# A routed choice in single slots, rows fetched earlier, and the last product of an expert turned ahead of the next hidden layer

## The chip, the cores and the metric

The kernel runs on one core of one Trainium2 chip. The metric is the time of one launch on the device, in microseconds (us); lower is better. Engines are named as the profile names them: PE (matrix products; PEld is its weight load), DVE (vector), ACT (scalar), POOL (GpSimd) and SP, which here only issues DMAs.

## What is computed

Three layers run one after the other on 1536 tokens of width 512 (2 batches of 768 tokens):

```python
# 1. attention inside clusters: 8 heads of 64, 16 clusters per head
q_assign = argmax(q_n @ c_n.T); k_assign = argmax(k_n @ c_n.T)
scores = where(q_assign[:, None] == k_assign[None, :], q @ k.T / 8, -1e9)
x = softmax(scores) @ v                      # -> 1536 x 512
# 2. one of 8 experts for every token, 512 -> 1024 -> 512
e = argmax(x @ w_gate)
y = softmax(x @ w_gate)[e] * sigmoid(x @ w_output_gate[:, e]) * (relu(x @ w1[e]) @ w2[e])
# 3. dense layer, 512 -> 2048 -> 512
h = y @ w_in
out = (h * sigmoid(1.702 * h)) @ w_out
```

## The kernel before, in words

**Attention** (about 25 to 262 us of the span) is a loop of 96 steps written out by hand (line 939 on), one step for 128 queries of one head. In a step PE makes the scores (L515, L516), DVE finds the row maximum (`nm`, L518), ACT takes the exponential (L524), PE transposes the result (L532) and ACT and DVE copy one half each out of PSUM (`pT`, L537 and L539). Every engine works through its instructions in the order in which the program issues them.

**Routing** is a Python generator, `route(gi)` (L606 on), run for three groups of tokens: the 768 of the first batch, then twice 384 of the second. The loop takes it one `yield` further four times in a step, so its small DVE instructions fall between those of attention. For group 0 it also makes the *choice* (L670 to L690): 18 DVE instructions on tiles of 128x8 or less that find the largest expert of the first half, its number and its first row (`soon`), and how many of its tokens, at most `FIRST` = 128, are worked on early. The rank sums (`prk`) lie in a PSUM slot that PE's `pox` (L586) uses next; the slot comes free with `dest` (L691). After that POOL scales the rows by the gate (L725) and scatters them to the tensor `xd` (an indirect DMA, L730).

**The early expert.** `soon_at` (L921) says at which attention step its parts are issued: the number and the row (`soon_ids`, step 75), the weights in twelve DMAs (`soon_weights`, L760, steps 84 and 87), the 128 rows (`soon_rows`, L782, step 87, behind the last of the weights), and their transposes (`soon_x`, L790, step 91). All DMAs named so far but POOL's are issued by SP in this order. The products (L806, L816) run behind attention, at 267 to 284 us.

**Experts** (284 to 463 us). A conditional branch for overflowing experts (L1233, not taken here) comes first. Then experts 0 to 7 run with 304, 256, 224, 208, 192, 176, 160 and 128 rows. The rows of expert 0 are fetched behind the branch by `win_start(0, True)` (L1323; L1105) in three DMAs of 128, 128 and 48 rows; `win_x` transposes them (L1118) and splits them into a high part (ACT, L1122) and a low part (DVE, L1123). An expert has eight steps `g`, `c = g % 8`. In a step:

- a weight tile is split: ACT casts the high part (L1048), POOL subtracts the low part (L1051); where `g % 4 == 3`, DVE does that instead of POOL (`split_low`);
- `win_h` makes the hidden layer on PE (L1130 to L1132, or L1134 and L1135 where a tile holds high and low rows side by side). ACT copies half of the sums (`hs`, L1140), DVE adds the halves (L1141), ACT applies relu and gives the high part (`ht`, L1155), DVE gives the low part (L1158, `low`);
- `win_y` makes the second product of the step two before (L1134, L1135). With the last one of an expert, which falls into the step `c == 1` of the next expert, `win_out` adds the output (`hs` and `room`, four times L1140 and L1141), writes `yth` on ACT (L1182) and `ytl` on POOL (L1183).

The order of issue on DVE in such a step is: the total of `h` (L1141), the four of `room` if there are any, `split_low`, then `low`.

**The dense layer** (463 to 731 us) keeps PE busy throughout.

Of the kernel before, what the change touches and what calls it, by code (L numbers as in the profile page):

```python
# [9 lines left out]
F32 = mybir.dt.float32  # L10
# [4 lines left out]
ALU = mybir.AluOpType  # L15
# [4 lines left out]
B, H, S, D = 2, 8, 768, 64  # L20
C = 16
NT = B * S
DM = H * D
E = 8
# [22 lines left out]
def attention_moe_ffn(ctx: ExitStack, tc: tile.TileContext, q, k, v, centroids, w_gate, w_og, w1, w2, w_in, w_out, out):  # L47
    nc = tc.nc
    const = ctx.enter_context(tc.tile_pool(name="const", reuse_waits="tile", bufs=1))

    def f32(ap):
        return ap.bitcast(F32)
# [553 lines left out]
    def route(gi):  # L606
# [4 lines left out]
        def new(nm, shape, dt=F32):  # L611
            return one.tile(shape, dt, name=f"{nm}{gi}")
# [54 lines left out]
        if gi < len(GROUPS) - 1:  # L667
            lk = new("lk", [128, E])
        if gi == 0:
            nc.vector.scalar_tensor_tensor(lk, part, float(E), rev8, op0=ALU.mult, op1=ALU.add)  # L670
            lm, lv = new("lm", [128, 1]), new("lv", [128, E])
            nc.vector.tensor_reduce(lm, lk, op=ALU.max, axis=AX.X)
            nc.vector.tensor_scalar(soonh, lk, lm, None, op0=ALU.is_equal)
            yield
            nc.vector.tensor_tensor(lv, soonh, part, op=ALU.mult)
            nc.vector.tensor_reduce(ngone, lv, op=ALU.add, axis=AX.X)
            nc.vector.tensor_scalar(ngone, ngone, float(FIRST), None, op0=ALU.min)
            yield
            nc.vector.tensor_scalar(gone, soonh, ngone, None, op0=ALU.mult)
            nc.vector.scalar_tensor_tensor(sbase, gone, -1.0, ebase, op0=ALU.mult, op1=ALU.add)  # L680
            nc.vector.scalar_tensor_tensor(srev8, gone, -float(E), rev8, op0=ALU.mult, op1=ALU.add)
            yield
            nc.vector.tensor_tensor(lv, soonh, ebase, op=ALU.mult)
            nc.vector.tensor_reduce(span[:, 1:2], lv, op=ALU.add, axis=AX.X)
            nc.vector.tensor_tensor(span[:, 0:1], span[:, 1:2], ngone, op=ALU.subtract)
            yield
            nc.vector.tensor_tensor(lv, soonh, iota8, op=ALU.mult)
            nc.vector.tensor_reduce(lm, lv, op=ALU.add, axis=AX.X)
            nc.vector.tensor_copy(soon[:, 0:1], lm[0:1])
            nc.vector.tensor_copy(soon[:, 1:2], span[0:1, 0:1])  # L690
        nc.vector.tensor_tensor(dest, rk, sbase[:, None, :].to_broadcast([128, nj, E]), op=ALU.add)  # L691
        if gi == len(GROUPS) - 2:
            nc.vector.scalar_tensor_tensor(lk, part, float(E), srev8, op0=ALU.mult, op1=ALU.add)
        yield
# [223 lines left out]
    slots.update({21: 3, 27: 1, 75: 1, 80: 1, 81: 2, 86: 3, 87: 2, 92: 2, 93: 2})  # L918

    weights = soon_weights()  # L920
    soon_at = {75: [soon_ids], 84: [lambda: next(weights)], 87: [lambda: next(weights), soon_rows], 91: [soon_x]}  # L921

    fixed = ExitStack()
    fixed.enter_context(tc.manual_schedule())
# [170 lines left out]
    def win_load(ex_row, n, one_tile=False, pieces=False):  # L1095
        nr = -(-n // 128)
        if one_tile:
            x = hp.tile([128, 2 * CAP], F32R, name="ht", tag="ht")[:, None, :DM].bitcast(F32)
        else:
            x = xp.tile([128, WR, DM], F32, name="xr", tag="xr", bufs=1)  # L1100
        d = {"n": n, "nr": nr, "x": x}
        for r0 in range(0, nr, 1 if pieces else nr):
            m, p = (1, min(128, n - r0 * 128)) if pieces else (nr, 128)
            row = nc.s_assert_within(ex_row + r0 * 128, 0, E * NT - 128, skip_runtime_bounds_check_because="inside the rows of an expert") if r0 else ex_row
            x = nc.sync.dma_start(out=d["x"][:p, r0:r0 + m], in_=xd[bass.ds(row + FIRST, m * p)].rearrange("(r p) c -> p r c", p=p)).ins  # L1105
            need(x, scatters)
        return d

    def win_x(d, r):
        if r == 0:  # L1110

            side = CAPS.index(d["n"]) % 2 if d["n"] in CAPS else 0
            d["t"] = xp.tile([128, 8 * CAPS[side]], F32R, name="t", tag=f"t{side}", bufs=1)[:, :8 * d["n"]].rearrange("p (k n) -> p k n", k=4)
        m = min(128, d["n"] - r * 128)
# [5 lines left out]
        hi = d["t"][:, :, n + r * 128:n + r * 128 + m]  # L1120
        src = pt.rearrange("p (k n) -> p k n", k=4)[:, :, :m]
        nc.scalar.copy(hi, src)  # L1122
        nc.vector.tensor_tensor(d["t"][:, :, r * 128:r * 128 + m], src, f32(hi), op=ALU.subtract)  # L1123

    def product(ps, n, w_hi, w_lo, t, first, last):

# [81 lines left out]

    xp = cx.enter_context(tc.tile_pool(name="xp", reuse_waits="tile", bufs=2))
    hp = cx.enter_context(tc.tile_pool(name="hp", reuse_waits="tile", bufs=3))  # L1210

    wins = {}
# [10 lines left out]
    relus[1]()  # L1223
    low_parts.append(split_pair(ekeys[1], 0, None, nc.vector, True))
    some(100)
    for f in low_parts:
        f()
    trips = nc.values_load_multi_w_load_instructions(trip, min_val=0, max_val=NOV)[1][0]
# [91 lines left out]
            ahead[g] = ph  # L1320

    with tc.manual_schedule():
        win_start(0, True)  # L1323
        loads_to(6)
        banks.clear()
        banks.extend([(ps_m, "m"), (ps_t, "pt"), (ps_t, "pt"), (ps_a, "po")])
        for r in range(wins[0]["nr"]):
            win_x(wins[0], r)
        n_, half = order[2]
        split_pair(ekeys[n_], half)  # L1330
        exps += experts(plan[:, 1:E])
        dense_load(2)
        win_start(1)
        loads_to(7)
        G = E * 8
        hq = deque()
        for g in range(G + 2):
            e, c = divmod(g, 8)
            nxt = wins.get(e + 1)
            r = c - (7 - nxt["nr"]) if nxt else 0  # L1340
            split_low = low = out_low = None
            if g + 3 < len(order):
                n_, half = order[g + 3]
                split_low = split_pair(ekeys[n_], half, None, nc.vector if g % 4 == 3 else nc.gpsimd, g % 4 == 3)
                loads_to(g + 7)
            if nxt and 0 <= r < nxt["nr"]:
# [15 lines left out]
            if g >= 2:  # L1362
                g0, ht = hq.popleft()
                e0, c0 = divmod(g0, 8)
                win_y(wins[e0], ("e", e0, c0 // 2), c0 % 2, ht, c0 == 0, c0 == 7)
                if c0 == 7:

                    low_end = S // 8 + (e0 and (LEAST + (e0 - 1) * ((NT - FIRST - LEAST) // (E - 1))))
                    col = nc.s_assert_within(offs[e0], low_end, NT if e0 else FIRST, skip_runtime_bounds_check_because="a sum of counts")
                    out_low = win_out(wins[e0], col, True, nc.vector if e0 == E - 1 else None)  # L1370
            if split_low:
                split_low()
            for f in (low, out_low):
                if f:
                    f()
            dense_step(min(5 * e + max(0, c - 2), 40) + 3 * min(max(0, g - 61), 2))
            if g < G:
                if c == 0 and e and e + 1 < E:
                    win_start(e + 1)
                if g == 2:  # L1380
                    offs = nc.values_load_multi_w_load_instructions(plan[:, E:], engines=[ACT_E, DVE_E, POOL_E], min_val=0, max_val=NT)[1]
# [111 lines left out]
```

## Time and profile before

| | us |
|---|---|
| median of 3 runs (lowest, highest) | 731.31 (730.92, 732.39) |
| profiled execution | 733.72 |
| its span, first to last instruction | 732.0 |
| busy in the span: PE, DVE, ACT, POOL | 703.2, 458.1, 393.0, 264.4 |
| mean granted clock of PE | 0.985 of full speed |

PE is busy for 96% of the span, so the stretches in which it waits or runs at a lower granted clock are what can be won without taking work away. A time in brackets at the end of a row of a timeline is how long the engine had been idle before, and what released it. A number behind x is how many instructions a row stands for.

### The profile page before, as it was taken

The numbers are of one execution on the slowest core, as the hardware profiler recorded it, in microseconds if no ns is written. First come the engines' busy times: TensorE is split into PE (matmuls) and PEld (weight loads), VectorE is DVE, ScalarE is ACT, GpSimd is POOL, SyncE is SP. The second block draws the span as 40 slices with busy tenths as digits, with TensorE's granted clock in tenths as the row PEclk, the third lists the DMA queues.
The fourth block names the chain that finished last, engine by engine and source line by source line (L and its number), as shares of the span: only waits on it lengthen the run. The fifth ranks groups of instructions, "written<-read, shape, count | busy, mean of one in ns | idle before, by whom it ended". The sixth has DMA issues, their size and how long they took to land.

```text
span 732.0 us, 12543 instructions
## 1 busy us (share of the span) xinstructions
PE 703.2 (96%) x4522; PEld 580.2 (79%) x4522; DVE 458.1 (63%) x886; ACT 393.0 (54%) x789; POOL 264.4 (36%) x219
## 2 busy tenths in 40 slices
PE   8999999998999898999999897999999999999996
PEld 6776776776866678999999887888888888888885
DVE  6969788889888774344554545687655657232322
ACT  7767675675666544556777676544534344222120
POOL 2230330312750013755978889222432212020202
PEclk8999999999899999999999999999999999999999
DMA  6778969637274427766477776132643211010101
GB/s 195 171 189 266 238 216 293 142 121 173 69 200 141 174 86 255 230 215 215 161 254 243 236 224 222 59 116 86 68 73 41 81 59 56 1 58 1 58 0 58
DMA packets 70594, 105.18 MB, mean 144 GB/s; under 512 B 9648, under 2 KB 48304, under 8 KB 70528
## 3 DMA queue, kind: packets, MB, share of 16 engines
q1 hardware_dynamic: 67584, 95.94, 45.9%
q0 software_dynamic: 2944, 8.40, 3.0%
q8 instruction: 37, 0.61, 0.4%
q14 instruction: 29, 0.24, 0.1%
HBM read 70.46 MB, written 14.69 MB: 116 GB/s over the span
## 4 chain that ended last, share of the span: by engine, by line
PE 33%; issue 16%; ACT 5%; DVE 3%; POOL 2%; DMA 1%; POOLq 0%; ACTq 0%; DVEq 0%
PE ph L1317 4%; PE ph L1318 4%; PE ph L1319 4%; PE py L1412 3%; PE py L1411 3%; PE py L1410 3%; PE py L1134 3%; ACT w L1048 3%; PE ph L1134 3%; PE ph L1135 1%; PE py L1135 1%; DVE w L1051 1%; DMA raw<-in_moe_w_dram 1%; POOL out_dram L1421 1%; ACT hs L1140 1%
## 5 line engine op out<-in xcount | busy, mean ns | idle before, releaser
L1051 POOL TENSOR_TENSOR w<-raw,w 128x1024 fp32r<-128x1024 f32 x51 | 125.6, 2482 | 39.3 <-ACT w L1048 38.9
L518 DVE TENSOR_REDUCE nm<-sp 128x1 f32<-128x768 f32 x96 | 91.6, 955 | 16.2 <-PE sp L516 14.1
L1395 DVE TENSOR_TENSOR sg<-ph,sg 128x512 f32<-128x512 f32 x48 | 33.2, 691 | 99.7 <-ACT sg L1394 97.5
L524 ACT ACTIVATE P<-sp,nm 128x768 f32<-128x768 f32 x96 | 87.2, 908 | 11.3 <-DVE nm L518 10.6
L532 PEld LDWEIGHTS pt<-ident,P 128*128 128x128 f32 x576 | 66.4, 143 | 28.1 <-issue 17.5
L532 PE MATMUL pt<-ident,P 128*128 128x128 f32 x576 | 84.3, 280 | 4.0 <-ACT pT L537 2.1
L1394 ACT ACTIVATE sg<-ph 128x512 f32<-128x512 f32 x48 | 28.7, 597 | 104.7 <-PE ph L1319 100.3
L1134 PE MATMUL py<-ht,w 128*128 128x512 f32 (+6 forms) x224 | 70.2, 367 | 8.0 <-DVE ht L1158 5.1
L515 PE MATMUL sp<-X,Q 128*128 128x384 f32 x192 | 74.9, 390 | 0.5 <-ACT P L524 0.4
L1412 PE MATMUL py<-w,gl 128*128 128x512 f32 (+1 forms) x194 | 75.2, 387 | 0.0
L1411 PE MATMUL py<-w,gh 128*128 128x512 f32 (+1 forms) x194 | 75.1, 387 | 0.0
L1410 PE MATMUL py<-w,gh 128*128 128x512 f32 (+1 forms) x194 | 75.0, 387 | 0.0
L1317 PE MATMUL ph<-yth,w 128*128 128x512 f32 x192 | 74.8, 390 | 0.0
L1318 PE MATMUL ph<-ytl,w 128*128 128x512 f32 x192 | 74.7, 389 | 0.0
L1319 PE MATMUL ph<-yth,w 128*128 128x512 f32 x192 | 74.7, 389 | 0.0
L1084 POOL TENSOR_TENSOR w<-csq,w 128x512 fp32r<-128x512 f32 x24 | 32.7, 1364 | 115.7 <-ACT w L1083 115.7
L1048 ACT CAST w<-raw 128x1024 fp32r<-128x1024 f32 x68 | 70.5, 1042 | 4.2 <-issue 2.4
L1134 PE MATMUL ph<-t,w 128*128 128x512 f32 (+6 forms) x224 | 69.4, 365 | 0.4 <-DVE ht L1158 0.4
L567 PE MATMUL po<-pT,ld_v 128*32 128x384 f32 x768 | 69.0, 492 | 0.0
L516 PE MATMUL sp<-Z,Q 80*128 80x384 f32 x192 | 66.4, 346 | 0.5 <-DMA Q<-ohT 0.5
L537 ACT COPY pT<-pt 128x384 f32<-128x384 f32 x96 | 45.8, 477 | 36.8 <-PE pt L532 36.8
L539 DVE COPY pT<-pt 128x384 f32<-128x384 f32 x96 | 52.8, 550 | 12.6 <-PE pt L532 12.2
(291 smaller groups left out, 1476.2 us busy)
## 6 DMA issues: line engine op xcount, KB each, us to landing
raw<-in_moe_w_dram SPq DMA_DIRECT2D x64, 512.0 KB, 4.5
raw<-in_moe_w_in_dram SPq DMA_DIRECT2D x16, 512.0 KB, 4.1
raw<-in_moe_w_out_dram SPq DMA_DIRECT2D x16, 512.0 KB, 4.8
xd<-zrow SPq DMA_DIRECT2D x8, 768.0 KB, 5.9
Q<-Hq SPq DMA_DIRECT2D x28, 192.0 KB, 2.7
ew<-in_moe_w_dram SPq DMA_DIRECT2D x9, 384.0 KB, 7.8
ld_q<-in_q_dram SPq DMA_DIRECT2D x8, 384.0 KB, 6.0
ld_k<-in_k_dram SPq DMA_DIRECT2D x8, 384.0 KB, 3.8
```

The source lines that it names most:

```text
L518: nc.vector.tensor_reduce(nm, sp[:, :, :384], op=ALU.max, axis=AX.XY, negate=True)
L524: nc.scalar.activation(P, L["sp"][:, :, :384], AF.Exp, bias=L["nm"], accum_out=L["sm"][:, h, j % 3:j % 3 + 1])
L532: nc.tensor.transpose(pt[:, r * 128:(r + 1) * 128], L["P"][:, n, r * 128:(r + 1) * 128], ident)
L1048: nc.scalar.copy(hi, r)
L1051: (eng or nc.gpsimd).tensor_tensor(lo, r, f32(hi), op=ALU.subtract)
L1134: nc.tensor.matmul(ps[:, :2 * n], w_hi, t, start=first, stop=False)
L1317: nc.tensor.matmul(ph, wa(key, 0, k, i), yth[:, k, cs], start=(k == 0), stop=False)
L1318: nc.tensor.matmul(ph, wa(key, 0, k, i), ytl[:, k, cs], start=False, stop=False)
L1319: nc.tensor.matmul(ph, wa(key, 1, k, i), yth[:, k, cs], start=False, stop=(k == 3))
L1410: nc.tensor.matmul(po[m][:, cs], gh[:, ms], wb(key, 0, i)[:, cs], start=first, stop=False)
L1411: nc.tensor.matmul(po[m][:, cs], gh[:, ms], wb(key, 1, i)[:, cs], start=False, stop=False)
L1412: nc.tensor.matmul(po[m][:, cs], gl[:, ms], wb(key, 0, i)[:, cs], start=False, stop=last)
```

## The change

- **Choice.** `dest` for group 0 is now written first, from the rank sums and `ebase` alone, and the counts are copied from PSUM to `c0`; every instruction of the choice after that stands in a slot of its own, and at the end `gone` is subtracted from `dest`. Two DVE instructions are added. The generator has twelve more `yield`s, three steps' worth.
- **Early rows.** `soon_rows` moves from the end of step 87 to the front of step 84, ahead of the weights; `soon_ids` moves from step 75 to 78.
- **First rows of expert 0.** The DMA of its first 128 rows is issued ahead of the branch (and waits for the scatters of groups 0 and 1 alone); behind the branch one DMA brings the other 176 as two tiles of 88. `xr` gets a pool of its own, `xrp`.
- **Experts.** In the steps `c == 1` from g = 9 to 57 the last `win_y` of the expert before, with its additions, is issued ahead of that step's `win_x` and `win_h`. In every step `low` is issued ahead of `split_low`. `yth` and `ytl` are still issued last.

```diff
@@ route(0)
-            nc.vector.scalar_tensor_tensor(lk, part, float(E), rev8, op0=ALU.mult, op1=ALU.add)
-            lm, lv = new("lm", [128, 1]), new("lv", [128, E])
+            nc.vector.tensor_tensor(dest, rk, ebase[:, None, :].to_broadcast([128, nj, E]), op=ALU.add)
+            lm, lv, c0 = new("lm", [128, 1]), new("lv", [128, E]), new("c0", [128, E])
+            nc.vector.tensor_copy(c0, part)
+            yield
+            nc.vector.scalar_tensor_tensor(lk, c0, float(E), rev8, op0=ALU.mult, op1=ALU.add)
+            yield
             nc.vector.tensor_reduce(lm, lk, op=ALU.max, axis=AX.X)
+            yield
...
+            yield
+            nc.vector.tensor_tensor(dest, dest, gone[:, None, :].to_broadcast([128, nj, E]), op=ALU.subtract)
+        else:
+            nc.vector.tensor_tensor(dest, rk, sbase[:, None, :].to_broadcast([128, nj, E]), op=ALU.add)
@@ soon_at
-    soon_at = {75: [soon_ids], 84: [lambda: next(weights)], 87: [lambda: next(weights), soon_rows], 91: [soon_x]}
+    soon_at = {78: [soon_ids], 84: [soon_rows, lambda: next(weights)], 87: [lambda: next(weights)], 91: [soon_x]}
@@ win_load
+        if pieces:
+            p = (n - 128) // (nr - 1)
+            d["rows"] = [128] + [p] * (nr - 1)
+            rows_of(0, 1, 128, scatters[:-GROUPS[-1][2]])
+            d["rest"] = lambda: rows_of(1, nr - 1, p, scatters)
+        else:
+            rows_of(0, nr, 128, scatters)
@@ ahead of the branch, and behind it
     some(100)
+    win_start(0, True)
     for f in low_parts:
...
-        win_start(0, True)
+        wins[0]["rest"]()
@@ experts
+            turned = c == 1 and 1 < g < G
+            if turned:
+                finish()
             if nxt and 0 <= r < nxt["nr"]:
                 win_x(nxt, r)
...
-            if split_low:
-                split_low()
-            for f in (low, out_low):
+            if g >= 2 and not turned:
+                finish()
+            for f in (low, split_low, *late):
```

`finish` holds what stood at the place of the old `if g >= 2:`: `win_y` of the step two before and, for the last of an expert, the additions of `win_out`.

## Rows read from the trace of the kernel before

**Rows 1.** Waits of PE, whole span: line, releaser, total us, times, longest.

```profile
PE py L1134 <- DVE ht L1158: 5.1, 5, 2.3
PE py L1134 <- DVE room L1141: 2.7, 4, 0.7
PE pxs L790 <- DMA xs<-xd: 2.4, 1, 2.4
PE pxt L1118 <- issue: 1.4, 1, 1.4
```

**Rows 2.** Windows: PE, PEld, DVE, ACT, POOL busy (instructions), clock, DMA share, GB/s.

```profile
170.00:180.00 10.00, 8.51 (x80) 5.45 (x72) 9.44 (x29) 5.00 (x13) 0.56 (x1) 1.00 0.88 214
180.00:190.00 10.00, 9.23 (x49) 7.58 (x53) 8.46 (x28) 4.63 (x10) 3.90 (x3) 0.66 0.07 26
190.00:200.00 10.00, 10.00 (x88) 7.56 (x81) 8.30 (x15) 7.34 (x17) 8.90 (x9) 1.00 0.31 101
```

**Rows 3.** Timeline of DVE around the choice: start, duration, line, operation.

```profile
178.69 0.16 DVE L670 SCALAR_TENSOR_TENSOR lk<-prk,rev 128x8 f32<-128x8 f32 x1
...
179.80 0.55 DVE L539 COPY pT<-pt 128x384 f32<-128x384 f32 x1
...
182.62 0.18 DVE L691 TENSOR_TENSOR dest<-prk,sbase 128x48 f32<-128x48 f32 x1
```

**Rows 4.** Timeline of PE in the same stretch.

```profile
180.31 0.81 PE L532 MATMUL pt<-ident,P 128*128 128x128 f32 x3 [1.01 <-ACT pT L537]
...
182.86 1.44 PE L586 MATMUL pox<-wo,oa 128*128 128x160 f32 x4 [0.45 <-DVE dest L691]
```

**Rows 5.** Timeline of POOL: the last scatter of group 0.

```profile
205.86 1.05 POOL L730 DMA_INDIRECT xd<-xs,di  x1 [0.28 <-POOL xs L725]
```

**Rows 6.** Timeline of SP's queue around the early expert.

```profile
229.19 4.61 SPq L760 DMA_DIRECT2D ew<-in_moe_w_dram  x7
...
239.66 0.34 SPq L782 DMA_DIRECT2D xs<-xd  x1
```

**Rows 7.** Windows where the early rows are waited for, columns as in rows 2.

```profile
246.00:248.00 2.00, 0.00 (x0) 0.00 (x0) 0.80 (x1) 0.12 (x2) 0.00 (x0) 1.00 0.16 58
248.00:254.00 6.00, 5.86 (x41) 3.69 (x42) 3.17 (x5) 2.48 (x5) 0.00 (x0) 0.72 0.00 0
```

**Rows 8.** Timeline of SP's queue behind the branch.

```profile
280.69 1.46 SPq L1105 DMA_DIRECT2D xr<-xd  x3
```

**Rows 9.** Timeline of PE behind the branch.

```profile
284.35 0.96 PE L1118 MATMUL pxt<-ident,xr 128*128 128x128 f32 x7 [0.40 <-PEq L1233]
286.74 0.70 PE L1118 MATMUL pxt<-ident,xr 128*128 128x128 f32 x5 [1.44 <-issue]
287.96 0.41 PE L1130 MATMUL ph<-t,w 128*128 128x304 f32 x1 [0.52 <-ACT t L1122]
```

**Rows 10.** The window behind those, columns as in rows 2.

```profile
288.00:294.00 6.00, 5.64 (x27) 5.42 (x28) 1.15 (x3) 3.58 (x5) 4.90 (x3) 0.72 0.97 321
```

**Rows 11.** Waits of ACT from 345 to 457 us, columns as in rows 1.

```profile
ACT ht L1155 <- DVE ph L1141: 26.1, 42, 2.2
ACT yth L1182 <- DVE room L1141: 2.6, 6, 0.5
```

**Rows 12.** A window late in the experts, columns as in rows 2.

```profile
430.00:451.00 21.00, 17.38 (x133) 16.69 (x133) 11.36 (x24) 14.41 (x32) 19.47 (x9) 1.00 0.66 206
```

**Rows 13.** Timeline of DVE: two of its weight splits and a low part.

```profile
361.18 2.38 DVE L1051 TENSOR_TENSOR w<-raw,w 128x1024 fp32r<-128x1024 f32 x1
363.48 0.38 DVE L1158 SCALAR_TENSOR_TENSOR ht<-ph,ht 128x224 fp32r<-128x224 f32 x1
...
382.60 1.22 DVE L1051 TENSOR_TENSOR w<-raw,w 128x1024 fp32r<-128x1024 f32 x1
```

**Rows 14.** All DVE splits, 345 to 457 us: busy total and mean ns, idle before.

```profile
L1051 DVE TENSOR_TENSOR w<-raw,w 128x1024 fp32r<-128x1024 f32 x11 | 21.7, 1974 | 0.0
```

**Rows 15.** Timeline of POOL: the splits beside the first of rows 13.

```profile
355.35 7.12 POOL L1051 TENSOR_TENSOR w<-raw,w 128x1024 fp32r<-128x1024 f32 x3 [0.70 <-ACT w L1048]
```

More of the change, by code (lines that the diff above doesn't have):

```diff
@@ L669, in route @@
         if gi == 0:
-            nc.vector.scalar_tensor_tensor(lk, part, float(E), rev8, op0=ALU.mult, op1=ALU.add)
-            lm, lv = new("lm", [128, 1]), new("lv", [128, E])
+            nc.vector.tensor_tensor(dest, rk, ebase[:, None, :].to_broadcast([128, nj, E]), op=ALU.add)
[4 more added lines that the diff above has]
+            yield
             nc.vector.tensor_reduce(lm, lk, op=ALU.max, axis=AX.X)
+            yield
             nc.vector.tensor_scalar(soonh, lk, lm, None, op0=ALU.is_equal)
             yield
-            nc.vector.tensor_tensor(lv, soonh, part, op=ALU.mult)
+            nc.vector.tensor_tensor(lv, soonh, c0, op=ALU.mult)
+            yield
             nc.vector.tensor_reduce(ngone, lv, op=ALU.add, axis=AX.X)
+            yield
             nc.vector.tensor_scalar(ngone, ngone, float(FIRST), None, op0=ALU.min)
@@ L679, in route @@
             nc.vector.tensor_scalar(gone, soonh, ngone, None, op0=ALU.mult)
+            yield
             nc.vector.scalar_tensor_tensor(sbase, gone, -1.0, ebase, op0=ALU.mult, op1=ALU.add)
+            yield
             nc.vector.scalar_tensor_tensor(srev8, gone, -float(E), rev8, op0=ALU.mult, op1=ALU.add)
@@ L683, in route @@
             nc.vector.tensor_tensor(lv, soonh, ebase, op=ALU.mult)
+            yield
             nc.vector.tensor_reduce(span[:, 1:2], lv, op=ALU.add, axis=AX.X)
+            yield
             nc.vector.tensor_tensor(span[:, 0:1], span[:, 1:2], ngone, op=ALU.subtract)
             yield
+            nc.vector.tensor_copy(soon[:, 1:2], span[0:1, 0:1])
             nc.vector.tensor_tensor(lv, soonh, iota8, op=ALU.mult)
+            yield
             nc.vector.tensor_reduce(lm, lv, op=ALU.add, axis=AX.X)
+            yield
             nc.vector.tensor_copy(soon[:, 0:1], lm[0:1])
-            nc.vector.tensor_copy(soon[:, 1:2], span[0:1, 0:1])
-        nc.vector.tensor_tensor(dest, rk, sbase[:, None, :].to_broadcast([128, nj, E]), op=ALU.add)
+            yield
+            nc.vector.tensor_tensor(dest, dest, gone[:, None, :].to_broadcast([128, nj, E]), op=ALU.subtract)
+        else:
+            nc.vector.tensor_tensor(dest, rk, sbase[:, None, :].to_broadcast([128, nj, E]), op=ALU.add)
         if gi == len(GROUPS) - 2:
@@ L1099, in win_load, with rows_of @@
         else:
[L1100 to L1103, printed above, removed]
+            x = xrp.tile([128, WR, DM], F32, name="xr", tag="xr")
+        d = {"n": n, "nr": nr, "x": x, "rows": [128] * (nr - 1) + [n - 128 * (nr - 1)]}
+        def rows_of(r0, m, p, names):
             row = nc.s_assert_within(ex_row + r0 * 128, 0, E * NT - 128, skip_runtime_bounds_check_because="inside the rows of an expert") if r0 else ex_row
             x = nc.sync.dma_start(out=d["x"][:p, r0:r0 + m], in_=xd[bass.ds(row + FIRST, m * p)].rearrange("(r p) c -> p r c", p=p)).ins
-            need(x, scatters)
+            for nm in scatters[len(names):]:
+                tc.declare_no_dep(x, nm, reason="an expert with 128 rows in these groups: later tokens have other rows")
+            need(x, names)
+        if pieces:
+            p = (n - 128) // (nr - 1)
+            d["rows"] = [128] + [p] * (nr - 1)
+            assert sum(d["rows"]) == n and LEAST >= 128
+            rows_of(0, 1, 128, scatters[:-GROUPS[-1][2]])
+            d["rest"] = lambda: rows_of(1, nr - 1, p, scatters)
+        else:
+            rows_of(0, nr, 128, scatters)
         return d
@@ L1113, in win_x @@
             d["t"] = xp.tile([128, 8 * CAPS[side]], F32R, name="t", tag=f"t{side}", bufs=1)[:, :8 * d["n"]].rearrange("p (k n) -> p k n", k=4)
-        m = min(128, d["n"] - r * 128)
+        m, r0 = d["rows"][r], sum(d["rows"][:r])
         xs = d["x"][:m, r]
@@ L1119, in win_x @@
         n = d["n"]
-        hi = d["t"][:, :, n + r * 128:n + r * 128 + m]
+        hi = d["t"][:, :, n + r0:n + r0 + m]
         src = pt.rearrange("p (k n) -> p k n", k=4)[:, :, :m]
         nc.scalar.copy(hi, src)
-        nc.vector.tensor_tensor(d["t"][:, :, r * 128:r * 128 + m], src, f32(hi), op=ALU.subtract)
+        nc.vector.tensor_tensor(d["t"][:, :, r0:r0 + m], src, f32(hi), op=ALU.subtract)
     def product(ps, n, w_hi, w_lo, t, first, last):
@@ L1210, in attention_moe_ffn @@
     hp = cx.enter_context(tc.tile_pool(name="hp", reuse_waits="tile", bufs=3))
+    xrp = cx.enter_context(tc.tile_pool(name="xrp", reuse_waits="tile", bufs=1))
     wins = {}
@@ L1340, in attention_moe_ffn @@
             r = c - (7 - nxt["nr"]) if nxt else 0
-            split_low = low = out_low = None
+            split_low = low = None
+            late = []
             if g + 3 < len(order):
@@ L1345, in attention_moe_ffn, with finish @@
                 loads_to(g + 7)
+            def finish():
+                g0, ht = hq.popleft()
+                e0, c0 = divmod(g0, 8)
+                win_y(wins[e0], ("e", e0, c0 // 2), c0 % 2, ht, c0 == 0, c0 == 7)
+                if c0 == 7:
+                    low_end = S // 8 + (e0 and (LEAST + (e0 - 1) * ((NT - FIRST - LEAST) // (E - 1))))
+                    col = nc.s_assert_within(offs[e0], low_end, NT if e0 else FIRST, skip_runtime_bounds_check_because="a sum of counts")
+                    late.append(win_out(wins[e0], col, True, nc.vector if e0 == E - 1 else None))
+            turned = c == 1 and 1 < g < G
+            if turned:
+                finish()
             if nxt and 0 <= r < nxt["nr"]:
@@ L1361, in attention_moe_ffn @@
                 banks.append((ps_h, "ph"))
[L1362 to L1370, printed above, removed]
-            if split_low:
-                split_low()
-            for f in (low, out_low):
+            if g >= 2 and not turned:
+                finish()
+            for f in (low, split_low, *late):
                 if f:
```

## The prediction

> **What bounds the kernel now.** I read the waits of PE first, because PE is busy for 96% of the span and what it does not do elsewhere it does in the dense layer, where it never waits: a microsecond won ahead of that layer reaches the end. The reader is to see four places [rows 1]: the early rows (2.4 us, once), the transposes behind the branch (1.4), and two waits inside the experts, for the low part of `ht` (5.1 in five times) and for `room` (2.7 in four). The list does not show what the granted clock takes. So I read windows next. From 180 to 190 us the clock is 0.66, a loss of 10 x 0.34 = 3.4 us; PE was busy 8.51 of 10 before it, and DVE 9.44 of 10 [rows 2]. From 248 to 254 it is 0.72, 6 x 0.28 = 1.7 us lost, after two microseconds with PE at 0.00 [rows 7]. From 288 to 294 it is 0.72 again, another 1.7 us, behind the branch [rows 10]. In each, parts of the stretch run at 1.2 instead of 2.4 GHz. Last I read the waits of the engines that PE waits for, stage by stage, since a wait of PE may be the shadow of another engine's pace.
>
> **Choice in single slots.** The choice's first instruction starts at 178.69 and `dest` ends at 182.80 [rows 3], 4.1 us; a `pT` copy of 0.55 and a row maximum of nearly 1 us lie between, so the choice costs 2.6 us of DVE in its densest stretch. PE waits there 1.01 us for a chain that starts with a late DVE and 0.45 us for `dest` [rows 4]. The new order writes `dest` at once and copies the counts, so the second wait goes. But the whole 0.45 + 1.01 + 3.4 = 4.9 us cannot be won: DVE itself is idle for only 10 - 8.46 = 1.5 us of that window [rows 2], and it gets two instructions more, about 0.35 us together at the 0.16 and 0.18 us of such ones [rows 3]. If DVE has the same work to do there, the gain ends at 1.5 - 0.35 = 1.2 us. The twelve new slots move a part of it behind 190 us, where DVE is idle for 1.7 us in 10 [rows 2]; that sets the far end at about -2.7. On the other side the longer stretch meets the preparation of the next heads, and one more stall like that of rows 4 costs 1.5 us. I take -1.0 us, close to what DVE's idle time allows, with -2.7 and +1.5 as ends. Three steps later (a step is (262 - 25) / 96 = 2.5 us) come also POOL's scalings and scatters: the last ended at 206.91 [rows 5] and would end near 215, still 14 us ahead of the first DMA that needs them. I cost that at nothing; if POOL's casts for the next heads came late through it, it would be of the order of 0.5 to 1 us.
>
> **Early rows in front of the weights.** Before, SP issues seven and then five weight DMAs from 229.19 and the rows at 239.66 [rows 6]; PE stands until 248.14, 2.41 us, though it could have used them at 245.7. Issued first, at about 229.2, they have 16 us; even the 8.5 us that they took behind the weights would do. The weights are 0.34 us later, and the products that need them come 20 us later. So the 2.4 us go and with them the fall of the clock, 1.7: -4.1 us. DVE has 3.17 of 6 us to do there [rows 7], so it is not late next. If the clock fell all the same, -2.4 would be left.
>
> **First 128 rows ahead of the branch.** PE's last transposes start at 286.74, 1.44 us after the ones before, and the row names no releaser; I take it to be the last of three DMAs that SP issues in 1.46 us from 280.69 [rows 8, 9]. After, one DMA of 0.49 us remains, so the last piece is issued 1.0 us earlier, and the weights in SP's queue behind it too; with 128 rows out of the way I put the gain at 1.4 us, between that 1.0 and the 0.40 + 1.44 that PE waits. The clock's 1.7 us I leave out: waits of 0.5 us for ACT [rows 9] and the start behind the branch stay. New in SP's queue ahead of the branch is a wait for the scatters of groups 0 and 1; behind it stand only transfers that were issued behind the branch. Ends: 0, if PE waited for something else, such as its own instructions, and -3.5 with the clock. A loss of up to 1 us is possible if the new pool lies where attention's tiles are still in use and SP stands.
>
> **The experts.** At first sight all of 5.1 + 2.7 + 0.4 us goes: `low` no longer stands behind the split, and `room` is asked for a whole `win_h` earlier. But from 345 to 457 us ACT waits 26.1 us for DVE's totals, in all 42 steps, 0.62 us each, and no wait of ACT for PE is in that list [rows 11]; PE is busy only 17.38 of 21 us late in it [rows 12]. So the turn ACT, DVE, ACT sets the pace (weight cast, `hs`, total, relu), and PE's waits are its shadow; only what shortens that turn counts. (1) With the last product turned ahead, `yth` no longer waits for `room`: 6 times, 2.6 us [rows 11]. (2) `low` ahead of the split works both ways. A split that finds POOL free takes 1.22 us [rows 13]; one at 361.18 took 2.38, and POOL's third instruction beside it ended at 355.35 + 7.12 = 362.47 [rows 15]: 1.29 us of waiting and 1.09 of work. Its start does not matter then, and behind it the 0.38 us of `low` [rows 13] no longer delays the next total: -0.3 us. A free split instead starts 0.8 us later (relu and `low`), ends 2.0 us after the total, and ACT brings the next half after some 1.7: +0.3. Walked through one by one, the eleven splits (mean 1.97 us [rows 14]) give six gains of 0.2 to 0.3, two zeros and three losses of 0.2 to 0.4: -0.8. Together -3.4; I take -3.0, since POOL, 19.47 of 21 us busy [rows 12], follows ACT closely and takes some back. Ends: -8.2 and +5, both below.
>
> Whether a DVE split beside POOL waits or merely runs slower decides that step. The sum of 1.29 and 1.09 speaks for waiting. The Trainium skill, "SBUF — State Buffer", section "SBUF: two separate sides", has the rule for it: GpSimd and a VectorE instruction with two SBUF inputs take a shared port pair as an exclusive lock for a whole instruction. The row agrees with it. By the rule my -0.8 stands where POOL's instruction is under way, but where POOL's next one has just begun the lock turns against the later start; that is the second rival.
>
> **Sum.** -1.0 - 4.1 - 1.4 - 3.0 = -9.5 us on the profiled execution's 733.72: 724.2. That execution is 2.4 us above the median of the runs, 731.31, so the forecast is 731.31 - 9.5 = 721.8.
>
> **Rivals.** *All of PE's waits in the experts go*: for it speaks that each names the very instruction that is moved, against it that ACT never waits for PE there. The experts then give -8.2, the time 716.6. *The late split meets POOL's next instruction.* POOL's splits follow without a pause (three in 7.12 us, 2.37 each [rows 15]). A split that starts 0.8 us later and just misses its turn waits a full 2.4 us: 0.8 + 2.4 + 1.1 - 1.7 = 2.6 us on the next total, where today it is about 1.97 + 0.38 - 1.7 = 0.65, so +1.95 for each such step. The gains, 6.5 elsewhere and 2.6 for `yth`, are eaten from the fifth of the eight splits that run beside POOL, and with the sixth the kernel is slower. All eight: +15.6 - 2.6 - 6.5 = +6.5, 737.8. Half of them: about +5 in the experts, 730 to 732. Against it speaks that most splits have over 0.8 us of POOL's instruction still ahead of them. *The change does not do what it says*: the choice stalls PE in its new slots and the clock falls there, and PE waits behind the branch for something other than the rows. The first and third parts give nothing: -7.1, 724.2.
>
> **How the numbers follow.** A measurement of this kernel tells about 0.2% (1.5 us) from no change: faster is below 729.8, slower above 732.8. Forecast 0.48; change without its first and third effect 0.20; all waits gone 0.13; half of the splits caught 0.11; all caught 0.08. So faster 0.81, same 0.11, slower 0.08. The range goes from 714.5, under the best rival by a part of the clock behind the branch, to 729.5, where three splits are caught and the choice gives nothing.
>
> **What would show it.** Right: no wait of PE at `pxs` and a full clock from 246 to 254; `pox` waiting for no `dest`; the last transposes some 1.4 us earlier after the branch; no `yth` waiting for `room`; ACT's waits for totals hardly smaller, while PE's named releasers change and its idle time in the experts shrinks by 3, not 8. Wrong: DVE splits over 3 us in most of the eleven; a clock below 1 behind the choice again; a row maximum that PE waits for in the steps behind it; a new wait of SP ahead of the branch.

## The result, and the profile after

The changed kernel takes 722.85 us (median; 722.55 to 724.04), the kernel before, beside it, 731.85: a ratio of 0.9876, with a 95% interval of 0.9857 to 0.9895. It is 9.0 us faster, where 9.5 were forecast. Its profiled execution has a span of 722.3 us against 732.0, 9.7 less. The total hides that two of the four terms were wrong in opposite directions.

To see where the time went, the same instruction is looked up in both traces. First the kernel before, then the changed one: a row maximum of DVE just ahead of the choice, one of step 76 and one of step 84.

```profile
175.32 0.95 DVE L518 TENSOR_REDUCE nm<-sp 128x1 f32<-128x768 f32 x1
210.61 0.94 DVE L518 TENSOR_REDUCE nm<-sp 128x1 f32<-128x768 f32 x1
228.09 0.96 DVE L518 TENSOR_REDUCE nm<-sp 128x1 f32<-128x768 f32 x1
```

```profile
175.78 0.95 DVE L518 TENSOR_REDUCE nm<-sp 128x1 f32<-128x768 f32 x1
206.78 0.94 DVE L518 TENSOR_REDUCE nm<-sp 128x1 f32<-128x768 f32 x1
225.69 0.96 DVE L518 TENSOR_REDUCE nm<-sp 128x1 f32<-128x768 f32 x1 [1.44 <-PE sp L516]
```

The first pair stands 0.46 us apart the wrong way (in the profiles of the kernels below, which are the same up to there, this row stands anywhere from 174.31 to 175.80, so stages are compared by differences). The second is 3.83 us earlier, the third only 2.40: the choice won 4.3 us, and 1.4 of them went back at step 84 in this execution. Next the changed kernel's timeline of PE behind the branch:

```profile
277.41 0.63 PE L1146 MATMUL pxt<-ident,xr 128*128 128x128 f32 x4 [0.40 <-PEq L1263]
278.81 0.45 PE L1146 MATMUL pxt<-ident,xr 88*128 88x88 f32 x3 [0.78 <-DMA xr<-xd]
280.14 0.99 PE L1146 MATMUL pxt<-ident,xr 88*128 88x88 f32 x5 [0.88 <-issue]
281.68 0.62 PE L1158 MATMUL ph<-t,w 128*128 128x304 f32 x1 [0.54 <-ACT t L1150]
```

and, by line, the first and last start of the first products of its dense layer, then the same of the kernel before:

```profile
L1347 PE MATMUL ph<-yth,w x192: 389/389/447, 453.2 to 706.7; 128*128 128x512 f32 x192
```

```profile
L1317 PE MATMUL ph<-yth,w x192: 389/389/447, 462.9 to 716.4; 128*128 128x512 f32 x192
```

Against [rows 9] the first transposes stand at 277.41 instead of 284.35, 6.94 us earlier, and the first product of the experts at 281.68 instead of 287.96, 6.28 earlier: the stretch behind the branch lost 0.7 us, and it was to win. The dense layer starts at 453.2 instead of 462.9. So 9.7 us are won by there, 3.4 of them in the experts, and none behind. The waits of PE in the changed kernel, as in [rows 1], and its windows that answer to [rows 2, 7, 10], columns as there:

```profile
PE py L1162 <- DVE room L1169: 2.0, 2, 1.4
PE sp L516 <- DMA Q<-ohT: 1.9, 2, 1.2
...
PE py L1162 <- DVE ht L1186: 1.1, 3, 0.6
...
PE pxt L1146 <- issue: 0.9, 1, 0.9
PE pxt L1146 <- DMA xr<-xd: 0.8, 1, 0.8
PE ph L1162 <- DVE ht L1186: 0.7, 2, 0.3
```

```profile
180.00:190.00 10.00, 9.35 (x79) 6.80 (x83) 9.72 (x35) 6.86 (x16) 0.00 (x0) 1.00 0.01 2
190.00:200.00 10.00, 10.00 (x87) 8.89 (x77) 9.11 (x18) 7.98 (x20) 6.45 (x6) 1.00 0.15 46
...
240.00:250.00 10.00, 10.00 (x92) 7.05 (x92) 9.08 (x14) 6.33 (x14) 0.00 (x0) 1.00 0.41 142
...
280.00:290.00 10.00, 9.32 (x47) 8.78 (x48) 2.60 (x5) 6.40 (x10) 7.31 (x4) 0.66 0.98 352
```

The reader is to see four things. The wait for the early rows is gone, and the clock is 1.00 where they were waited for. Behind the choice the clock is 1.00 and DVE is busier than before. A new wait for `Q<-ohT` of 1.2 us stands at step 84. And behind the branch PE still stops with no releaser named, and the clock is 0.66 for 10 us, a loss of 3.4 us.

### The profile page after: what moved, and what is told of

Read it like the earlier page. It is cut to its first block, busy times and chain, and to the rows that moved or that the text cites. A ratio compares the mean times of both kernels' runs of the same rounds, so it can differ in the third digit from the quotient of the medians.

```text
span 722.3 us, 12542 instructions
## 1 busy us (share of the span) xinstructions
PE 699.4 (97%) x4522; PEld 577.7 (80%) x4522; DVE 452.2 (63%) x888; ACT 393.0 (54%) x789; POOL 266.4 (37%) x219
## 4 chain that ended last, share of the span: by engine, by line
PE 54%; issue 17%; POOL 7%; DMA 7%; DVE 6%; ACT 6%; SPq 1%; POOLq 0%; ACTq 0%; DVEq 0%
PE po L567 6%; PE pt L532 5%; PE ph L1347 4%; PE ph L1349 4%; PE ph L1348 4%; PE py L1447 3%; PE py L1445 3%; PE py L1446 3%; PE sp L515 3%; PE sp L516 3%; POOL w L1067 3%; PE py L1162 3%; PE ph L1162 2%; ACT w L1064 2%; DMA raw<-in_moe_w_dram 2%
## 5 line engine op out<-in xcount | busy, mean ns | idle before, releaser
L1067 POOL TENSOR_TENSOR w<-raw,w 128x1024 fp32r<-128x1024 f32 x51 | 128.1, 2529 | 38.3 <-ACT w L1064 25.4
```

What stands on the lines that cost most here:

```text
L1067: (eng or nc.gpsimd).tensor_tensor(lo, r, f32(hi), op=ALU.subtract)
```

## The experiments

The other kernels of the table are the changed one with one edit, but for `changed_again`, which has none, and `loads_held_old_rows`, which has two. Times are medians beside runs of the kernel before on the same chip; since those differ from one measurement to the next (731.9 to 733.8), the ratios are what can be compared.

| kernel | us | ratio to before (95%) | span |
|---|---|---|---|
| changed | 722.85 | 0.9876 (0.9857 to 0.9895) | 722.3 |
| changed_again | 723.65 | 0.9868 (0.9838 to 0.9897) | 722.2 |
| no_choice | 726.12 | 0.9903 (0.9871 to 0.9935) | 726.0 |
| no_early_rows | 728.64 | 0.9943 (0.9920 to 0.9967) | 727.1 |
| no_first_rows | 722.19 | 0.9855 (0.9825 to 0.9884) | 720.5 |
| no_branch | 719.47 | 0.9815 (0.9785 to 0.9844) | 718.1 |
| no_turn | 726.74 | 0.9908 (0.9884 to 0.9931) | 725.7 |
| no_low_first | 726.40 | 0.9894 (0.9865 to 0.9922) | 725.0 |
| choice_dest_first | 726.77 | 0.9906 (0.9877 to 0.9934) | 723.8 |
| transposes_ahead | 724.54 | 0.9874 (0.9850 to 0.9899) | 723.4 |
| loads_held | 726.24 | 0.9899 (0.9871 to 0.9928) | 724.3 |
| loads_held_old_rows | 727.91 | 0.9919 (0.9893 to 0.9945) | 729.2 |
| split_earlier | 719.45 | 0.9814 (0.9787 to 0.9842) | 718.7 |

The changed kernel stands at 0.987 in both of its measurements; 0.1% of the ratio is 0.73 us.

**The choice undone.**

```diff
-            nc.vector.tensor_tensor(dest, rk, ebase[:, None, :].to_broadcast([128, nj, E]), op=ALU.add)
...
-            nc.vector.tensor_copy(c0, part)
-            yield
...
+        nc.vector.tensor_tensor(dest, rk, sbase[:, None, :].to_broadcast([128, nj, E]), op=ALU.add)
```

> The changed kernel with the choice as it was before (up to seven DVE instructions in a slot, dest last); all else as changed. Theory of the traces: from the scores of step 64 to those of step 76 the changed kernel gained 4.3 us on the kernel before (3.3 by step 68) and gave 1.4 back at step 84, so without it the clock falls to about 0.66 from 180 to 190 us again, PE waits again for dest, its wait for Q<-ohT at step 84 goes from 1.2 back to about 0.5 us, and the kernel is about 3.2 us slower than the changed one: 726. Theory of the prediction (DVE's own idle time limits the gain): 1.0 us slower, 723.9.

0.3% slower, 2 to 2.6 us; the span is 3.7 longer. PE's timeline behind the choice, and the window:

```profile
183.25 1.97 PE L586 MATMUL pox<-wo,oa 128*128 128x160 f32 x6 [1.28 <-DVE dest L691]
```

```profile
180.00:190.00 10.00, 8.02 (x53) 6.61 (x57) 8.94 (x30) 5.08 (x12) 3.52 (x3) 0.83 0.04 14
```

The waits are back, 1.28 us for `dest` this time, and the clock falls, though for half as long (0.83, not 0.66). The theory of the traces is nearer than the prediction's 1.0 us, which the interval does not exclude.

**The choice with `dest` first, but in few slots** (twelve `yield`s taken out again).

```diff
             nc.vector.tensor_copy(c0, part)
-            yield
             nc.vector.scalar_tensor_tensor(lk, c0, float(E), rev8, op0=ALU.mult, op1=ALU.add)
-            yield
             nc.vector.tensor_reduce(lm, lk, op=ALU.max, axis=AX.X)
...
```

> The changed kernel with dest and the copy of the counts first, but the choice in as few slots as before. Theory A (what counts is that the PSUM slot of the rank sums comes free at once): no wait of PE for dest, a clock near 1 from 180 to 190 us, 722.9 as the changed kernel, and, with POOL's scatters three steps earlier, PE's wait for Q<-ohT at step 84 at 0.5 instead of 1.2 us. Theory B (what counts is that the choice is thinned out): PE waits 1.0 us for pT again, the clock falls, some 2 us slower, 725.

0.3 to 0.4% slower than the changed kernel, as theory B has it, though the intervals overlap at their ends. PE's timeline shows no wait for `dest`, but three for `pT`, and its window a full clock all the same:

```profile
180.47 0.55 PE L532 MATMUL pt<-ident,P 128*128 128x128 f32 x3 [1.00 <-ACT pT L537]
184.03 0.55 PE L532 MATMUL pt<-ident,P 128*128 128x128 f32 x3 [1.16 <-ACT pT L537]
186.49 0.55 PE L532 MATMUL pt<-ident,P 128*128 128x128 f32 x3 [0.87 <-DVE pT L539]
```

```profile
180.00:190.00 10.00, 7.51 (x59) 5.36 (x60) 9.63 (x31) 4.72 (x11) 3.52 (x3) 1.00 0.04 16
```

From the row maximum of step 64 to that of step 76 this kernel takes 33.0 us, the changed one 31.0 and the one with the choice undone 33.9: in these profiles thinning out is worth 2.0 us, the slot that comes free early 0.9. So thinning out counts for more than the PSUM slot. No wait for `Q<-ohT` stands at step 84 here, nor in the other two kernels with few slots; whether the longer choice makes the 1.2 us of the changed kernel is taken up with its second profile.

**The early rows behind the weights again.**

```diff
-    soon_at = {78: [soon_ids], 84: [soon_rows, lambda: next(weights)], 87: [lambda: next(weights)], 91: [soon_x]}
+    soon_at = {78: [soon_ids], 84: [lambda: next(weights)], 87: [lambda: next(weights), soon_rows], 91: [soon_x]}
```

> The changed kernel with the DMA of the early rows behind the early weights again; all else as changed. Theory: PE waits some 2.4 us at the transposes of the early rows and the granted clock falls behind that, 1.7 us: 4.1 us slower than the changed kernel, 727. Rival: the fall of the clock had to do with what came before it, not with this wait: 2.4 us slower, 725.2.

0.7% slower, about 5 us. The wait is 3.2 us (PE has become earlier, the rows have not), and the clock falls; a wait of PE, then the window:

```profile
PE pxs L806 <- DMA xs<-xd: 3.2, 1, 3.2
```

```profile
240.00:250.00 10.00, 6.83 (x50) 4.91 (x49) 4.80 (x8) 3.89 (x8) 0.00 (x0) 0.83 0.30 105
```

3.2 and 10 x 0.17 = 1.7 are 4.9 us. The theory holds, the rival falls.

**The first rows behind the branch again, and the branch left out.**

```diff
-    win_start(0, True)
     for f in low_parts:
...
-        wins[0]["rest"]()
+        win_start(0, True)
...
```

> The changed kernel with the rows of expert 0 fetched by three DMAs behind the branch, as before; all else as changed. Theory of the prediction (the landing of the rows sets the last transposes): they come about 1.4 us later, the kernel is some 1.4 us slower than the changed one, 724.2. Rival from the traces (in both kernels PE stops in front of the eighth transpose behind the branch with no releaser named, whatever rows it needs, so it is PE's own instructions that are late; the new order only adds a wait of 0.78 us for the 88-row tiles and makes the stretch of low clock 6.8 instead of 3.4 us long): the gap in front of the eighth transpose stays, the wait for xr is gone, and the kernel is about 1 us faster than the changed one, 721.9.

```diff
-        with tc.If(trips > 0):
-            with tc.For_i(0, trips):
...
```

> The changed kernel without the branch and the loop behind it that work on overflowing experts (left out; with these inputs no expert overflows). Theory (PE's instructions behind the branch come late): the 0.40 us at the first transpose and the 0.88 us in front of the eighth are gone, a wait for the rows of 0.8 us or somewhat more stays; 1.3 us faster than the changed kernel if the clock falls all the same, 721.5, and up to 4.7 us faster, 718.2, if it does not. Rival (the rows are late): the gap in front of the eighth transpose stays, at most 0.4 us faster, 722.4.

PE's timeline behind the branch with the old order of rows; then at the same place where there is no branch, and that kernel's window:

```profile
275.71 0.95 PE L1134 MATMUL pxt<-ident,xr 128*128 128x128 f32 x7 [0.41 <-PEq L1249]
279.03 0.70 PE L1134 MATMUL pxt<-ident,xr 128*128 128x128 f32 x5 [2.36 <-issue]
```

```profile
277.41 0.80 PE L1146 MATMUL pxt<-ident,xr 88*128 88x88 f32 x8 [1.23 <-DMA xr<-xd]
278.80 0.40 PE L1158 MATMUL ph<-t,w 128*128 128x304 f32 x1 [0.59 <-ACT t L1150]
```

```profile
280.00:290.00 10.00, 10.00 (x73) 10.00 (x73) 2.02 (x4) 5.78 (x10) 9.48 (x4) 1.00 0.97 352
```

Seven transposes run, then PE stops, in the kernel before [rows 9], in the changed one (four and three) and in the one with the old order; the eighth belongs to the second tile, whose other three have just run, so it cannot be the rows. Without the branch all eight of the second and third tile run in one go, the waits there without a releaser are gone, the clock stays at 1.00, and the kernel is 0.55% faster, some 4 us. With the old order it is as fast as the changed kernel within the intervals. The rows ahead of the branch bring nothing that shows.

**All rows and transposes ahead of the branch.**

```diff
     win_start(0, True)
+    wins[0]["rest"]()
     for f in low_parts:
         f()
...
+    for r in range(wins[0]["nr"]):
+        win_x(wins[0], r)
...
```

> The changed kernel with all rows of expert 0 and their twelve transposes and copies ahead of the branch. Theory (PE's own instructions come late behind the branch, in any order): the gap without a releaser is still there, now behind the first products, ACT's and DVE's copies lie beside it, the clock falls less; 2.5 us faster than the changed kernel, 720.4. Rival (the rows' landing, near 277 us, sets the end): PE waits for them ahead of the branch and for its instructions behind it, no gain, 722.9.

No gain. PE waits 1.21 us ahead of the branch, in front of the same eight transposes for which it waits 1.23 where there is no branch (there the row names the rows, here SP's queue), and behind the branch far longer than ever:

```profile
276.92 0.80 PE L1146 MATMUL pxt<-ident,xr 88*128 88x88 f32 x8 [1.21 <-SPq L1270]
282.99 0.59 PE L1158 MATMUL ph<-t,w 128*128 128x304 f32 x1 [5.27 <-PEq L1270]
```

SP had passed the branch first and issued four weight tiles from 277.15. That suggested that PE's instructions queue behind them, which the next two kernels test.

**The weights held back until the transposes are done.**

```diff
...
-        loads_to(6)
...
+        held.append(wins[0]["last"])
+        loads_to(6)
```

`held` names the last transpose, and the next load waits for it.

> The changed kernel, but SP issues the weight loads behind the branch only when PE has done its twelve transposes there. Theory (PE's instructions behind the branch are fetched by the same DMA engines and queue behind the weight loads): the gap without a releaser in front of the eighth transpose, 0.9 to 2.7 us so far, falls below 0.5 us, the first products come 1 to 2 us earlier, the clock falls less or not at all, and the weights have slack enough; 1 to 4 us faster than the changed kernel. Rival (the fetch takes its time whatever else is moved): the gap stays, the weights come later, same or up to 2 us slower.

> As the run with held loads, but with the rows of expert 0 fetched by three DMAs behind the branch, as before. Theory: without weights in the queue the fetch competes with 0.6 MB of rows alone; the gap is near that of the run with held loads, and the time within 1 us of it, since the placing of the first 128 rows matters little. Rival (the rows ahead of the branch do help once the fetch is out of the way): 1.5 us slower than the run with held loads.

The rival holds. PE's timeline of the first, with the gap and the wait that the late weights cause; its window around the gap; then the gap in the timeline of the second:

```profile
277.91 0.60 PE L1149 MATMUL pxt<-ident,xr 88*128 88x88 f32 x5 [1.46 <-issue]
...
287.84 0.41 PE L1161 MATMUL py<-ht,w 128*128 128x304 f32 x1 [1.40 <-ACT ht L1186]
```

```profile
276.00:278.00 2.00, 0.55 (x5) 0.37 (x5) 0.69 (x1) 0.58 (x1) 0.00 (x0) 1.00 0.00 0
```

```profile
280.31 0.70 PE L1137 MATMUL pxt<-ident,xr 128*128 128x128 f32 x5 [1.96 <-issue]
```

The gap is still 1.46 us with a DMA share of 0.00 beside it, so the weights' traffic is not what makes it. Holding them only makes them late: in the traces the stretch from PE's first product of the experts to the dense layer grows from 171.5 us to 176.0, and to 178.2 with the old order of rows, in part by a lower clock. By the times these kernels are 0.25 and 0.45% slower; the first interval overlaps that of the changed kernel, the second touches it.

**The changed kernel once more.**

> The changed kernel once more, with a second profile, beside the two runs with held loads. Expected: 722.9 or 0.9876 of the kernel before; the gap behind the branch somewhere between 0.9 and 2.7 us, as in the other kernels that have the same order there, and the stretch of low clock behind it 3.4 or 6.8 us long. If the length of that stretch is the same as in the first profile, it belongs to the new order; if it is 3.4, it is chance.

PE's timeline, the window, and the row maximum of step 84:

```profile
280.19 0.60 PE L1146 MATMUL pxt<-ident,xr 88*128 88x88 f32 x5 [2.48 <-issue]
```

```profile
280.00:290.00 10.00, 8.98 (x53) 8.59 (x54) 2.98 (x6) 6.34 (x10) 7.64 (x4) 0.83 0.86 298
```

```profile
224.50 0.96 DVE L518 TENSOR_REDUCE nm<-sp 128x1 f32<-128x768 f32 x1 [0.23 <-PE sp L516]
```

The gap is 2.48 us where it was 0.88, and the clock costs 1.7 us where it cost 3.4. Both sizes are chance of the execution. So is the wait at step 84: it is missing here, and the row maximum keeps 4.1 of the 4.3 us, although POOL's last scatter of the group starts at 216.15 in both profiles. In the eleven profiles with the choice in single slots this wait is missing once and otherwise 0.3 to 1.5 us long; in the three with few slots it is missing. So it was seen with the longer choice alone, but its size is not the choice's.

**The experts' two edits, each undone.**

```diff
-            turned = c == 1 and 1 < g < G
+            turned = False
```

> The changed kernel with the last product of an expert behind the next hidden layer again (low still ahead of the split); all else as changed. Theory of the prediction: yth waits for room again, 6 times, 2.6 us together, 725.5 if ACT sets the pace. Rival (only PE's own waits for room count, 2.7 before and 2.0 after): 0.7 us slower, 723.6.

```diff
-            for f in (low, split_low, *late):
+            for f in (split_low, low, *late):
```

> The changed kernel with DVE's split ahead of low again (the turn stays); all else as changed. Theory of the prediction: DVE's splits begin 0.8 us earlier and last longer (mean near 1.97 instead of 1.45 us), and the kernel is 0.8 us slower, 723.7. Rival (PE's waits for the low part are a loss of their own; they fell from 5.5 to 1.8 us): 3.7 us slower, 726.6.

0.35 and 0.2% slower, the second within the intervals, so the traces have to tell. From PE's first product of the experts to the first of the dense layer the kernel before takes 462.9 - 288.0 = 174.9 us, the changed one 453.2 - 281.7 = 171.5, the one without the turn 456.6 - 281.4 = 175.2, the one with the split first 455.8 - 281.0 = 174.8. Where both edits stand and the weights are not held back it is 170.2 to 172.3 us in all eight profiles; with one edit alone it is no shorter than before. What PE waited for without the turn, and what ACT waited for there from 335 to 450 us; then PE's wait with the split first, and DVE's splits by line in that kernel from 338 to 450 us:

```profile
PE py L1162 <- DVE room L1169: 7.1, 5, 2.9
```

```profile
ACT yth L1210 <- DVE room L1169: 2.6, 6, 0.5
```

```profile
PE py L1162 <- DVE ht L1186: 7.7, 5, 3.1
```

```profile
L1067 DVE TENSOR_TENSOR w<-raw,w 128x1024 fp32r<-128x1024 f32 x11 | 21.5, 1954 | 0.1
```

With `low` first alone the waits for `ht` are gone and those for `room` have grown to 7.1 us; with the turn alone it is the other way round, 7.7 for `ht`. Both of these kernels wait about as long as the kernel before (5.1 + 2.7 + 0.4); only the pair brings it down to 2.0 + 1.1 + 0.7.

That does not make each alone worthless. POOL's fifth `ytl`, in the kernel before, in the second profile of the changed one, without the turn, and with the split first:

```profile
431.31 1.71 POOL L1183 TENSOR_TENSOR ytl<-room,yth 128x704 f32 x1 [0.47 <-ACT yth L1182]
422.14 1.72 POOL L1211 TENSOR_TENSOR ytl<-room,yth 128x704 f32 x1 [0.17 <-PE ph L1163]
423.89 1.71 POOL L1211 TENSOR_TENSOR ytl<-room,yth 128x704 f32 x1 [0.38 <-ACT yth L1210]
422.78 1.71 POOL L1211 TENSOR_TENSOR ytl<-room,yth 128x704 f32 x1 [0.26 <-ACT yth L1210]
```

From PE's first product (287.96, 281.39, 281.37 and 280.98) that is 143.4, 140.8, 142.5 and 141.8 us, and the clock behind the branch cost 1.7 us in each. By there the pair has won 2.6 us and one edit alone 0.9 or 1.6. Alone, the gain is lost after that, in one wait of 2.9 or 3.1 us and in the clock, which falls behind it; the windows from 438 to 450 us without the turn and with the split first:

```profile
438.00:450.00 12.00, 9.06 (x53) 8.91 (x53) 6.41 (x15) 7.41 (x18) 10.71 (x6) 0.72 0.61 218
438.00:450.00 12.00, 10.86 (x70) 10.86 (x71) 6.22 (x16) 7.29 (x18) 9.97 (x5) 0.72 0.68 218
```

That is 12 x 0.28 = 3.4 us, where the profile before lost nothing and the second one of the changed kernel 1.7. So it stays open whether the two gains add up: by the times, undoing the turn costs 2.3 to 2.9 us and undoing the other 1.3 to 1.9.

**DVE's weight splits one step earlier.**

```diff
-                split_low = split_pair(ekeys[n_], half, None, nc.vector if g % 4 == 3 else nc.gpsimd, g % 4 == 3)
+                split_low = split_pair(ekeys[n_], half, None, nc.vector if g % 4 == 2 else nc.gpsimd, g % 4 == 2)
```

> The changed kernel, but DVE makes its weight splits at g % 4 == 2 instead of 3, so that none of them stands in the step just ahead of an expert's end. Theory (what PE still waits for in the experts, 3.8 us, comes from DVE's splits that POOL holds up near the ends of the late experts, the longest at 436.66 us with 2.51): the longest wait, 1.4 us for room, goes, the waits in the experts fall to about 2 us, 1 to 2 us faster than the changed kernel. Rival (POOL is as full as before, so the collisions only move): the sum of the waits stays near 3.8 us, same time within 0.5 us.

PE's wait in the experts, and DVE's splits by line from 338 to 450 us:

```profile
PE py L1162 <- DVE ht L1186: 2.6, 3, 1.8
```

```profile
L1067 DVE TENSOR_TENSOR w<-raw,w 128x1024 fp32r<-128x1024 f32 x11 | 14.8, 1343 | 0.0
```

The theory holds in the main: no wait for `room` is left, the waits of 3.8 us are 2.6 where it named 2, the stretch from the first product to the dense layer takes 449.6 - 280.2 = 169.4 us, less than in any of the eight, and the kernel is at 0.9814. Its interval misses that of the changed kernel's first measurement and overlaps the second's by a hair. The span is 3.5 us shorter than either, but only 2.1 to 2.3 us of that lie in the experts; the rest lies ahead of them, where nothing was edited.

## Why the prediction was right, and where it was not

The forecast was 721.8 and the time 722.85. By its own steps:

**The choice: mis-sized, -1.0 forecast, 2 to 3 us measured.** The profile gives 4.3 - 1.4 = 2.9 us against the kernel before, the undone kernel 2 to 2.6 by its time and, by step 76, 2.9 in its profile. The step that failed is the bound: "If DVE has the same work to do there, the gain ends at 1.5 - 0.35 = 1.2 us." It took DVE's idle time from the one window in which PE stood still. What DVE can use is the idle time as far as the slots reach: from 180 to 200 us it was idle for 1.54 + 1.70 = 3.2 us before [rows 2] and for 0.28 + 0.89 = 1.2 after. The far end of -2.7, which was worked out that way, was the better value. The cost put at nothing, what comes three steps later, was not always nothing: a wait for `Q<-ohT` of 1.2 us came up, and the row maximum of step 84 lost 1.4. The text had 0.5 to 1 us for it, if POOL's casts came late; but POOL's scatters stand at the same time in the second profile, where the wait is missing, so POOL alone does not make it, and what does stays open.

**The early rows: right.** -4.1 forecast; 4.9 us by the trace of the kernel without it, 0.7% by its time.

**The first rows: wrong, -1.4 forecast, nothing measured.** The step that failed is "I take it to be the last of three DMAs". The row named no releaser, and the pause falls in front of the eighth transpose in all but two of the fourteen profiles, whichever rows it needs; the two are the one without the branch, where it is gone, and the one with the transposes ahead, where it stands in front of the first product. The case stood among the ends ("its own instructions") and as half of the last rival, and the packets shown in the last section bear it out. In the profile of the changed kernel the stretch even lost 0.7 us, but its gap and its clock are within what executions of one order differ by.

**The experts: the total right (-3.0 forecast, -3.4 measured), its parts not settled.** The text gave 2.6 us to the turn and 0.8 to `low`, as if they added up. In its profile each alone has won 0.9 or 1.6 us by the fifth `ytl` and nothing at the dense layer, where a long wait and the clock have taken it back; by the times, which the noise blurs, undoing them costs 2.3 to 2.9 and 1.3 to 1.9. The reading that PE's waits "are its shadow" was half wrong: PE's own end starts the dense layer, so its waits are the loss, 8.2 us before and 4.3 after (with 0.5 for `t` in `ph`), a difference of 3.9, of which 3.4 reach that layer. Half right it was in that they did not all vanish: ACT still waits 25.4 us for totals, 44 times, against 26.1 in [rows 11]. Its row, from 335 to 448 us, and DVE's splits by line from 338 to 450, both of the changed kernel:

```profile
ACT ht L1183 <- DVE ph L1169: 25.4, 44, 1.9
```

```profile
L1067 DVE TENSOR_TENSOR w<-raw,w 128x1024 fp32r<-128x1024 f32 x11 | 16.0, 1454 | 0.0
```

The rival with splits caught by POOL's next instruction did not come: DVE's splits are shorter, 1.45 us in the mean against 1.97 [rows 14], since in seven of the eleven, at 1.21 to 1.27, POOL is through with its own or within 0.2 us of it. One that starts at 355.05, while POOL works until 355.51, takes 1.55: 0.46 of waiting and 1.09 of work, as in [rows 13, 15]. The Trainium skill's rule of the exclusive lock ("SBUF — State Buffer", "SBUF: two separate sides") leaves both outcomes open; these rows agree with it. In the kernel with splits one step earlier the mean is 1.34.

That the total came out within 1 us is in part luck: the choice won 1 to 2 us more and the first rows 1.4 us less than forecast.

## What to carry to other kernels

A row that names no releaser is not evidence for the nearest transfer: see which instruction the pause stands in front of, whether its neighbours with the same inputs have run, and whether a packet of kind `instruction` comes in just before its end. Two queues that delay the same engine are best mended together: with one edit alone the waits came back under the other's name (7.1 and 7.7 us), so a term for each is no safe forecast. Bound what a busy engine can absorb over the whole reach of the new slots, not over the window in which it hurts now.

## What the hardware showed that was not expected

Behind the branch that is not taken PE waits 0.40 us, executes seven transposes, and stops again for 0.9 to 2.8 us. The stop stays with a DMA share of 0.00 beside it (1.46 us) and is gone without the branch and the loop that it jumps over. In the kernel with the transposes ahead the first stop was 5.27 us.

The DMA view shows what ends it. It counts packets by queue and kind, and queue 8 has packets of the kind `instruction`, 0.02 MB each. In the dense layer, where PE never waits, one starts for every 120 to 136 products; behind the branch one starts out of turn. Its line in a window of 0.25 us around its start (number, MB, and the time that it took as a share of 16 DMA engines), from 277.50 us in the changed kernel:

```profile
q8 instruction: 1, 0.02, 33.0%
```

It took 0.330 x 16 x 0.25 = 1.32 us. For five profiles, in us:

| kernel | packet starts | it took | PE's stop ends | behind the packet's end |
|---|---|---|---|---|
| before | 283.78 | 1.68 | 286.74 | 1.3 |
| changed | 277.51 | 1.32 | 280.14 | 1.3 |
| changed_again | 277.84 | 0.94 | 280.19 | 1.4 |
| loads_held | 275.44 | 1.01 | 277.91 | 1.5 |
| transposes_ahead | 280.31 | 0.93 | 282.99 | 1.8 |

In the other eight profiles with the branch the stop ends 1.3 to 1.5 us behind the packet's end as well. Without the branch no such packet starts from 270 to 282 us, and there is no stop. So PE waits for its own instructions; this is read from the traces, and no run moved the packet by itself. The packet starts from 0.6 us ahead of the first transpose behind the branch to 2.0 us behind it and takes 0.9 to 2.0 us, which together set the length of the stop; why it starts when it does stays open.

The granted clock that follows is not a steady price: the same order lost 1.7 us in one execution and 3.4 in another, and behind the choice 3.4, 1.7 and, with the longest waits of all, nothing. Late in the experts it fell again in the second profile of the changed kernel, by 1.7 us, and not in the first.
